# A fused attention and two-mixture kernel: the widest score tiles contract over all 128 rows of the array, and VectorE makes all low parts of the first mixture's weights

## The chip, the cores and the metric

The kernel runs on one core of a Trainium2 chip. A core has a matrix engine (PE; its weight loads are shown apart as PEld), three engines that work on tiles in on-chip memory (VectorE is DVE, ScalarE is ACT, GpSimd is POOL) and SyncE (SP), which here issues most of the transfers. The metric is the device time of one execution in microseconds; lower is better. The clock of the matrix engine has two levels: a granted clock of 1.00 in the profile is 2.4 GHz, 0.50 is 1.2 GHz.

## The reference

Three layers follow one another:

```python
# attention: q, k, v are (4, 8, 576, 64); blocks of 64 positions, a block sees itself and those before it
scores = (q @ k.T) / 8, masked to block_i >= block_j
attn = exp(scores - max) / (sum + 1e-9);  x = attn @ v        # -> x is (2304, 512)
# first mixture: rows with x @ w_skip > 0 go to the best of 8 experts by x @ w_gate
y = relu(x @ w1[e]) @ w2[e];  x = x + gate * y                # 512 -> 1024 -> 512
# second mixture: all rows through all 4 experts, weighted by normalised domain_probs
out = sum over e of p[:, e] * (relu(x @ w1[e]) @ w2[e])
```

All is float32 outside. Inside, an operand is split into a high part (rounded to a narrower form) and a low part (what the rounding left), and a product is three matmuls: high by high, high by low, low by high.

## The kernel before, in words

The program has three stages, which a hand-written order fixes (the scheduler is off: each engine runs its instructions as the code records them).

**Attention** runs over 8 units u, each a batch and a group of four heads. A unit's q is split into the tiles `QH` and `QL`, its k into `KH` and `KL`, each 128 partitions by 2 by 576: the heads of even number lie in partitions 0 to 63, those of odd number in 64 to 127, and the axis of length 2 is `h // 2`. So the contraction of one head, over 64 values, uses 64 of the 128 rows of the array. The score rows of a head are cut into five row tiles rt = 0 to 4; tile rt has 64 + 128 rt columns, so rt = 4 is the widest, with all 576. `score` makes one group: four heads for rt < 2, two heads for rt = 2 or 3, and one head for rt = 4. Where a group has two or four heads, their matmuls are issued in pairs, one on the lower and one on the upper 64 rows. For rt = 4 there is one head in a group, as two halves of 288 columns with three matmuls each, and a mask matmul of 64 columns: seven matmuls, all on the same 64 rows. Four such groups make 28 matmuls in a unit, 224 in all.

After `score`, VectorE takes the row maxima and ScalarE the exponentials (`E`). Two ways then turn `E`: for rt = 1 and 3 PE transposes it (`tp`, L303) and ScalarE and VectorE split it; for rt = 0, 2 and 4 ScalarE rounds `E` to `HL` (L309), GpSimd subtracts the low part (L310), and SyncE's queue issues a transposing transfer to `eT` (L311). Products with v (L335 to L337) follow some groups later, by a table of lags. While unit u is scored, the next unit's q, k and v are split, a few steps at a time: the string `SO` sets the order (J, K, Q on ScalarE; V on VectorE; q, k, v, the low parts `QL`, `kl`, `vl`, on GpSimd; a dot ends a step). Unit 0 has its own string, `S0`.

**The first mixture** (`m1`) goes through 8 experts. An expert's weights come as 8 pieces of 128 by 1024 (four of w1, then four of w2) into raw buffers; `sp` splits a piece as soon as it is its turn: the engines come from the table `SPE`, whose pair names the engine of the high part and that of the low part. In each expert ScalarE makes all high parts; VectorE makes the low parts of pieces 0 to 4 and 6, GpSimd those of pieces 5 and 7 (L635). A piece's raw buffer is free for the next load when its low part is done. On VectorE's queue the subtractions stand ahead of the splits of the transposed activations (`lo`, L658), which PE needs: it has two buffers for transposes (L665), so a third transpose of an expert's tile waits for the first `lo`. GpSimd's queue also issues the writes of the routed rows (L711).

**The second mixture** (`m2`) takes 807 us of the span, and neither edit touches it.

Of the kernel before, what the change touches and what calls it, by code (L numbers as in the profile page):

```python
# [6 lines left out]
F32 = mybir.dt.float32  # L7
F32R = mybir.dt.float32r
# [9 lines left out]
B, H, S, D = 4, 8, 576, 64  # L18
# [34 lines left out]
class Kernel:  # L53
# [5 lines left out]
    R3 = 4, 2  # L59
    CM = 6  # L60
    XO = 0
    S0 = "Qa0213b...V.v"
    XP = 2
    XB = 4
    YL = 5, 0
# [6 lines left out]
    LT = 99  # L72
    XQ = 3
    FT = (10,)
    SPE = ("AV", "AV", "AV", "AV", "AV", "AP", "AV", "AP")
    SB = 3
    PU, W2, X2 = 4, 1, 2
    ORD = "OSMDRTVPUE"
# [24 lines left out]
    PW = 2  # L103
    PM = 1
    HV = ((7, 0),)
    SO = "J..K..Q.Vq..k...v"

    def __init__(self, tc, q, k, v, wr, w11, w12, w21, w22, dp, out):
        self.tc, self.nc = tc, tc.nc
# [3 lines left out]
    def consts(self, cp, ac):  # L113
        nc, self.cp = self.nc, cp
        self.ident = cp.tile([128, 128], F32, name="ident")
        make_identity(nc, self.ident)

        self.maskl = ac.tile([128, 128], F32R, name="maskl")
        self.maskr = ac.tile([128, 64], F32R, name="maskr")
        nc.vector.memset(self.maskl.bitcast(F32), 0.0)  # L120
        nc.vector.memset(self.maskr.bitcast(F32), 1.0)
        for p in (0, 64):
            nc.vector.memset(self.maskl.bitcast(F32)[p:p + 1, 0:64], -1e9)
        self.ones = ac.tile([128, 128], BF16, name="ones")
        nc.vector.memset(self.ones, 1.0)
        tri = ac.tile([128, 128], F32, name="tri")
        nc.vector.memset(tri, 1.0)
        nc.gpsimd.affine_select(out=tri, in_=tri, pattern=[[1, 128]], base=-1, channel_multiplier=-1,
                                compare_op=ALU.is_ge, fill=0.0)
        self.tri = ac.tile([128, 128], BF16, name="tri16")  # L130
        nc.vector.tensor_copy(self.tri, tri)
        self.iota = ac.tile([128, 5, E1], F32, name="iota")
        self.plan = [(w, i, e, c) for e in range(E1) for i, w in enumerate((self.w11, self.w12)) for c in range(4)]
        self.plan += [(w, i, 0, c) for c in range(2) for i, w in enumerate((self.w21, self.w22))]
        self.raw1, self.done1, self.w, self.room = [], 0, [], self.RB
        self.hist = ac.tile([128, E1 + 1], BF16, name="hist")
        self.base = ac.tile([128, E1 + 1], BF16, name="base")
        nc.vector.memset(self.hist, 0.0)
        nc.vector.memset(self.base, 0.0)
        for e in range(E1 + 1):  # L140
            if e < E1:
                nc.gpsimd.memset(self.iota[:, :, e:e + 1], float(e - E1))
            nc.gpsimd.memset(self.base[0:1, e:e + 1], float(e * N))
        self.w9 = ac.tile([128, 4, E1 + 1], F32, name="w9")
        nc.sync.dma_start(self.w9, self.wr)
        self.tok = cp.tile([128, NT], I32, name="tok")
        nc.gpsimd.iota(self.tok, pattern=[[128, NT]], base=0, channel_multiplier=1)
        self.cnt = cp.tile([128, E1], I32, name="cnt")
        self.beg = cp.tile([128, E1], I32, name="beg")
        self.ful = cp.tile([128, E1], I32, name="ful")  # L150
        self.row = cp.tile([128, self.CM, E1], I32, name="row")

    def attention_consts(self, cp, kp):
        nc = self.nc
        self.vh, self.vl, self.kh, self.kl = [], [], [], []
        for i in range(2):
            for x, xs in (("h", self.kh), ("l", self.kl)):
                xs.append(kp.tile([128, 2, S], F32R, name=f"k{x}{i}"))
        for i in range(3):
            t = cp.tile([128, 5, 4, D + 1], F16, name=f"vh{i}")  # L160
            nc.gpsimd.memset(t[:, :, :, D:D + 1], 1.0)
            for h in range(4):
                nc.gpsimd.memset(t[64 - 64 * (h % 2):128 - 64 * (h % 2), 4 - 4 * (h % 2), h, D:D + 1], 0.0)
            self.vh.append(t)
            self.vl.append(cp.tile([128, 5, 4, D], BF16, name=f"vl{i}"))
# [18 lines left out]
    def split_unit(self, u):  # L184

        nc = self.nc
        qr, kr, vr = self.raws.pop(u)
        QH = self.qk.tile([128, 2, S], F32R, name="QH")
        QL = self.qk.tile([128, 2, S], F32R, name="QL")
        KH, KL = self.kh[u % 2], self.kl[u % 2]  # L190
        vh, vl = self.vh[u % 3], self.vl[u % 3]
        self.units[u] = (QH, QL, KH, KL, vh, vl)
        V = nc.vector
        what = {
            "Q": lambda: nc.scalar.copy(QH, qr),
            "q": lambda: (V if self.QV else nc.gpsimd).tensor_tensor(QL, qr, QH.bitcast(F32), ALU.subtract),
            "V": lambda: V.tensor_copy(vh[:, :, :, 0:D], vr),
            "v": lambda: (V if self.VV else nc.gpsimd).tensor_tensor(vl, vr, vh[:, :, :, 0:D], ALU.subtract),
        }
        if u:  # L200
            what["J"] = lambda: nc.scalar.mul(kr, kr, 0.125)
            what["K"] = lambda: nc.scalar.copy(KH, kr)
            what["k"] = lambda: nc.gpsimd.tensor_tensor(KL, kr, KH.bitcast(F32), ALU.subtract)
        else:
            for x, y, i in (("0", "2", slice(0, 1)), ("1", "3", slice(1, 2))):
                what[x] = lambda i=i: V.tensor_scalar(KH[:, i], kr[:, i], 0.125, None, ALU.mult)
                what[y] = lambda i=i: V.scalar_tensor_tensor(KL[:, i], kr[:, i], 0.125, KH[:, i].bitcast(F32),
                                                             ALU.mult, ALU.subtract)
        for x in self.SO if u else self.S0:
            if x == ".":  # L210
                yield
            elif x in "ab":
                i = "ab".index(x)
                (V if i else nc.gpsimd).tensor_tensor(QL[:, i], qr[:, i], QH[:, i].bitcast(F32), ALU.subtract)
            else:
                what[x]()

    def score(self, item, g):

        nc = self.nc  # L220
        u, rt, heads = item
        QH, QL, KH, KL, vh, vl = self.units[u]
        R = 128 if rt else 64
        r0 = 64 + 128 * (rt - 1) if rt else 0
# [9 lines left out]
        for j in range(per):  # L234
            h = heads[g0 + j]
            k0 = 0 if h % 2 else S - n
            if rt == 4:
                outs = [(sp[:, c, 0:288], 288 * c, 288) for c in range(2)]
                views.append(sp[:, :, 0:288])
            elif rt < 2:  # L240
                outs = [(sp[:R, h % 2, (h // 2) * n:(h // 2) * n + n], 0, n)]
                views.append(outs[0][0])
            else:
                outs = [(sp[:, h % 2, 0:n], 0, n)]
                views.append(outs[0][0])
            lm = None if not rt else (len(outs) - 1 if h % 2 else 0)

            p, hp = slice(64 * (h % 2), 64 * (h % 2) + 64), h // 2
            ops = []
            for i, (o, c0, w) in enumerate(outs):  # L250
                c0 += k0
                q, k = (p, hp, slice(r0, r0 + R)), (p, hp, slice(c0, c0 + w))
                ops += [(o, QH[q], KH[k], True, False), (o, QH[q], KL[k], False, False),
                        (o, QL[q], KH[k], False, i != lm)]
                if i == lm:
                    ops.append((o[:, w - 64:w] if h % 2 else o[:, 0:64], self.maskl[p], self.maskr[p], False, True))
            todo.append(ops)
        for two in range(0, per, 2):
            for ops in zip(*todo[two:two + 2]):
# [12 lines left out]
        for j in range(per):  # L272
# [3 lines left out]
            c = heads[j] % 2 * 2 + heads[j] // 2 if rt < 2 else j  # L276
# [448 lines left out]
    def sp(self, n, upto):  # L725
# [3 lines left out]
        for _ in range(n):  # L729
            m = self.done1  # L730
            if m >= min(upto, len(self.plan)):
# [4 lines left out]
            self.w[-1] += self.w_split(self.wp[0 if j < 3 else 1], f"{j}{m % 2}", self.plan[m][1], self.raw1[m],  # L736
                                       [en[c] for c in self.SPE[m % 8]])
            self.done1 += 1
# [407 lines left out]
```

## Time and profile before

| | us |
|---|---|
| runs | 1251.07, 1239.67, 1247.24 (median 1247.24) |
| profiled execution | 1245.87, of which the span is 1244.3 |

| stretch of the span, us | what runs | PE busy | DVE | ACT | POOL | granted clock |
|---|---|---|---|---|---|---|
| 42 to 215 | attention, past its start | 159.83 | 111.43 | 125.35 | 112.73 | 0.84 |
| 215 to 245 | end of attention, routing | 15.77 | 21.48 | 10.33 | 12.38 | 0.81 |
| 245 to 437 | first mixture | 164.00 | 100.22 | 92.25 | 55.53 | 0.95 |
| 437 to 1244 | second mixture | 780.27 | 567.42 | 258.06 | 422.54 | 0.99 |

Busy times are those of the engine in the stretch. PE's matmuls overlap and their ends are modelled, so a busy PE need not be one at its peak: how fast it goes is read from the distance between the starts of two matmuls, and from the granted clock. A busy figure beside a granted clock of 0.50 is time at 1.2 GHz.

### The profile page before, as it was taken

The page shows a single profiled execution, that of the slowest core. Times are in us where ns is not written, and L with a number is a line of the kernel's source. Part 1 is how long each engine was busy: PE and PEld are TensorE (multiplying, and loading weights), DVE is VectorE, ACT ScalarE, POOL GpSimd, SP SyncE. Part 2 cuts the span into 40 slices and gives each one's busy share as a digit, 9 for nine tenths or more (in the row PEclk, how much of TensorE's full clock was granted, in tenths as well). Part 3 has the DMA queues.
Part 4 walks back from the last instruction along what each step waited for, and adds up shares of the span by engine and source line. Part 5 has one row for each costly group of instructions (what it writes and reads, how often), then busy time and mean ns, then how long its engine had stood idle before and what let it go on. Part 6 is the DMA issues. An engine that isn't in the chain of part 4 may idle for free.

```text
span 1244.3 us, 21122 instructions
## 1 busy us (share of the span) xinstructions
PE 1145.9 (92%) x8105; PEld 1020.2 (82%) x8105; DVE 821.7 (66%) x1294; ACT 510.6 (41%) x900; POOL 627.2 (50%) x577
## 2 busy tenths in 40 slices
PE   4989999587898869999999999999999999999998
PEld 4878888576787758898998888988888888888887
DVE  4667566674434676766667766667876777667675
ACT  4887657365434553223232232323333232333321
POOL 4867665333112356554555445455755545555552
PEclk8898769798999979999999999999999999999999
DMA  5988648898553441111111111111411111111101
GB/s 180 207 187 191 170 104 162 236 331 291 165 182 100 137 153 52 51 35 35 34 52 37 49 35 35 51 35 58 129 52 51 52 52 51 35 51 52 35 1 68
DMA packets 129882, 123.89 MB, mean 100 GB/s; under 512 B 65965, under 2 KB 98733, under 8 KB 129744
## 3 DMA queue, kind: packets, MB, share of 16 engines
q1 hardware_dynamic: 127024, 117.48, 33.1%
q0 software_dynamic: 2720, 4.64, 1.1%
q8 instruction: 79, 1.29, 0.4%
q14 instruction: 59, 0.48, 0.1%
HBM read 91.83 MB, written 19.43 MB: 89 GB/s over the span
## 4 chain that ended last, share of the span: by engine, by line
PE 45%; DVE 9%; issue 5%; ACT 4%; POOL 2%; DMA 0%; SPq 0%; POOLq 0%; DVEq 0%; ACTq 0%
PE yp L641 9%; PE yp L643 9%; PE yp L642 8%; PE hp L642 6%; PE hp L643 6%; PE hp L641 6%; DVE acc L961 3%; DVE tl L874 2%; ACT hh L906 2%; DVE C L899 2%; ACT vh L870 1%; POOL C L899 1%; POOL p L899 1%; PE tp L820 1%; DVE u L899 0%
## 5 line engine op out<-in xcount | busy, mean ns | idle before, releaser
L906 ACT ACTIVATE hh<-C 128x512 fp32r<-128x512 f32 (+1 forms) x128 | 87.8, 686 | 434.5 <-DVE C L899 369.8
L641 PE MATMUL yp<-vh,hh 128*128 128x512 f32 x576 | 228.9, 397 | 11.0 <-ACT hh L906 11.0
L961 DVE SCALAR_TENSOR_TENSOR acc<-yp,p,acc 128x512 f32<-128x512 f32 x270 | 196.5, 741 | 56.5 <-PE yp L643 56.5
L643 PE MATMUL yp<-vh,hl 128*128 128x512 f32 x576 | 227.4, 395 | 0.3 <-DVE hl L907 0.3
L642 PE MATMUL yp<-vl,hh 128*128 128x512 f32 x576 | 227.6, 395 | 0.0
L907 DVE SCALAR_TENSOR_TENSOR hl<-C,hh 128x512 fp32r<-128x512 f32 (+1 forms) x128 | 120.9, 944 | 116.6 <-ACT hh L906 116.6
L899 POOL TENSOR_TENSOR p<-u,p 128x384 f32<-128x384 f32 (+1 forms) x64 | 60.2, 941 | 204.1 <-ACT p L896 204.1
L643 PEld LDWEIGHTS yp<-vh,hl 128*128 128x128 f32 x576 | 108.2, 188 | 31.9 <-DVE hl L907 8.2
L641 PEld LDWEIGHTS yp<-vh,hh 128*128 128x128 f32 x576 | 108.9, 189 | 27.5 <-ACT hh L906 14.5
L899 POOL TENSOR_TENSOR C<-u,p 128x384 f32<-128x384 f32 (+1 forms) x64 | 53.2, 831 | 148.0 <-ACT p L896 95.1
L642 PEld LDWEIGHTS yp<-vl,hh 128*128 128x128 f32 x576 | 108.9, 189 | 12.4
L642 PE MATMUL hp<-xsl,th 128*128 128x256 f32 (+1 forms) x384 | 113.6, 296 | 0.0
L643 PE MATMUL hp<-xsh,tl 128*128 128x256 f32 (+1 forms) x384 | 113.5, 296 | 0.0
L641 PE MATMUL hp<-xsh,th 128*128 128x256 f32 (+1 forms) x384 | 113.4, 295 | 0.0
L896 ACT COPY p<-hp 128x256 f32<-128x256 f32 (+1 forms) x192 | 74.5, 388 | 91.1 <-PE hp L643 91.1
L310 POOL TENSOR_TENSOR HL<-E,HL 128x640 bf16<-128x640 f32 (+2 forms) x39 | 66.0, 1704 | 54.8 <-ACT HL L309 45.5
L899 DVE TENSOR_TENSOR C<-hp,p 128x256 f32<-128x256 f32 (+1 forms) x128 | 57.5, 449 | 52.9 <-POOL p L899 52.9
L877 POOL TENSOR_TENSOR vl<-r,vh 128x1024 fp32r<-128x1024 f32 x31 | 91.3, 2945 | 0.0
L874 DVE TENSOR_TENSOR tl<-t,th 128x512 fp32r<-128x512 f32 x32 | 87.0, 2718 | 0.8 <-ACT th L872 0.8
L270 DVE TENSOR_REDUCE m<-s 128x1 f32<-128x576 f32 (+3 forms) x80 | 64.9, 819 | 26.8 <-PE s L261 26.2
L277 ACT ACTIVATE E<-s,m 128x320 f32<-128x320 f32 (+4 forms) x160 | 75.8, 532 | 15.1 <-DVE m L270 13.8
L641 PE MATMUL hp<-xdh,dh 128*128 128x256 f32 (+1 forms) x256 | 76.2, 297 | 1.9 <-ACT xdh L826 1.2
(199 smaller groups left out, 3095.5 us busy)
## 6 DMA issues: line engine op xcount, KB each, us to landing
r<-in_w_dram SPq DMA_DIRECT2D x128, 512.0 KB, 4.3
XN<-x SPq DMA_DIRECT2D x18, 256.0 KB, 7.1
x<-XN SPq DMA_DIRECT2D x18, 256.0 KB, 3.3
vr<-in_v_dram SPq DMA_DIRECT2D x7, 640.0 KB, 8.0
xg<-XS SPq DMA_DIRECT2D x16, 257.0 KB, 4.3
out_dram<-acc SPq DMA_DIRECT2D x16, 256.0 KB, 2.0
qr<-in_q_dram SPq DMA_DIRECT2D x7, 576.0 KB, 5.5
kr<-in_k_dram SPq DMA_DIRECT2D x7, 576.0 KB, 6.5
```

What stands on the lines that cost most here:

```text
L277: nc.scalar.activation(e, views[j], AF.Exp, bias=m[:R, c:c + 1])
L310: (nc.vector if item[:2] in self.HV else nc.gpsimd).tensor_tensor(HL[:R, w:2 * w].bitcast(BF16), Et[:R, 0:w], HL[:R, 0:w], ALU.subtract)
L641: nc.tensor.matmul(out, lhsT=ah, rhs=bh, start=start, stop=False)
L642: nc.tensor.matmul(out, lhsT=ah, rhs=bl, start=False, stop=False)
L643: nc.tensor.matmul(out, lhsT=al, rhs=bh, start=False, stop=stop)
L874: V.tensor_tensor(tl[:, 0:2], t[:, 0:2], th[:, 0:2].bitcast(F32), ALU.subtract)
L877: P.tensor_tensor(vl, r2, vh.bitcast(F32), ALU.subtract)
L896: nc.scalar.copy(t, product(a, b))
L899: add = lambda e, o, x, y: e.tensor_tensor(o, x, y, ALU.add)
L906: nc.scalar.activation(hh[:, i:i + 2], C[:, i:i + 2], AF.Relu)
L907: V.scalar_tensor_tensor(hl[:, i:i + 2], C[:, i:i + 2], 0.0, hh[:, i:i + 2].bitcast(F32), ALU.max, ALU.subtract)
L961: nc.vector.scalar_tensor_tensor(a, yp, self.p[:, n, e:e + 1], a, ALU.mult, ALU.add)
```

## The change

Two edits. **The widest tiles (rt = 4).** Each unit keeps, beside `QH` and `QL`, two tiles `q4h` and `q4l` of 128 partitions by 4 heads by 128 positions, with the last 128 positions of q: a head's 64 values stand in its own half of the partitions, and the other half holds zeros. There are two sets, for units in turn; GpSimd zeroes them once at the start and then copies, for each unit, the four pieces (steps X and x of the strings, each with two copies of 64 by 2 by 128). The rt = 4 matmuls take `q4h` and `q4l` as stationary operand and all 128 partitions of k as moving one; the rows of the other head meet zeros. Their mask matmul contracts over 128 rows too (`mask4`, with -1e9 in row 0 alone). The number, order and columns of the matmuls stay.

**The first mixture.** `SPE` now names VectorE for the low parts of pieces 5 and 7.

```diff
-    S0 = "Qa0213b...V.v"
+    S0 = "Qa0213b...V.vXx"
-    SPE = ("AV", "AV", "AV", "AV", "AV", "AP", "AV", "AP")
+    SPE = ("AV", "AV", "AV", "AV", "AV", "AV", "AV", "AV")
-    SO = "J..K..Q.Vq..k...v"
+    SO = "J..K..Q.Vq..k...vX.x"
...
-        for p in (0, 64):
-            nc.vector.memset(self.maskl.bitcast(F32)[p:p + 1, 0:64], -1e9)
+        self.mask4 = ac.tile([128, 128], F32R, name="mask4")
+        nc.vector.memset(self.mask4.bitcast(F32), 0.0)
+        for t, p in ((self.maskl, 0), (self.maskl, 64), (self.mask4, 0)):
+            nc.vector.memset(t.bitcast(F32)[p:p + 1, 0:64], -1e9)
...
+        self.q4 = []
+        for i in range(2):
+            self.q4.append([kp.tile([128, 4, 128], F32R, name=f"q4{x}{i}") for x in "hl"])
+            for t in self.q4[i]:
+                nc.gpsimd.memset(t.bitcast(F32), 0.0)
...
+        def last(x):
+            for a in range(2):
+                p = slice(64 * a, 64 * a + 64)
+                nc.gpsimd.tensor_copy(self.q4[u % 2][x][p].rearrange("p (c a) s -> p a c s", a=2)[:, a], (QH, QL)[x][p, :, S - 128:S])
+
+        what["X"], what["x"] = lambda: last(0), lambda: last(1)
...
-                q, k = (p, hp, slice(r0, r0 + R)), (p, hp, slice(c0, c0 + w))
-                ops += [(o, QH[q], KH[k], True, False), (o, QH[q], KL[k], False, False),
-                        (o, QL[q], KH[k], False, i != lm)]
+                if rt < 4:
+                    q, k = (p, hp, slice(r0, r0 + R)), (p, hp, slice(c0, c0 + w))
+                    qh, ql, ml, mr = QH[q], QL[q], self.maskl[p], self.maskr[p]
+                else:
+
+                    k = (slice(0, 128), hp, slice(c0, c0 + w))
+                    (qh, ql), ml, mr = (t[:, h] for t in self.q4[u % 2]), self.mask4, self.maskr
+                ops += [(o, qh, KH[k], True, False), (o, qh, KL[k], False, False), (o, ql, KH[k], False, i != lm)]
                 if i == lm:
-                    ops.append((o[:, w - 64:w] if h % 2 else o[:, 0:64], self.maskl[p], self.maskr[p], False, True))
+                    ops.append((o[:, w - 64:w] if h % 2 else o[:, 0:64], ml, mr, False, True))
```

What this does to the order of two queues follows. First GpSimd, around the split of the next unit in the middle of the attention (`QL`, `kl`, `vl`: the low parts of the next unit; `HL`: the low parts of E of the unit being scored). Before:

```order
L310 TENSOR_TENSOR HL<-E,HL 64x256
L196 TENSOR_TENSOR QL<-qr,QH 128x1152
L203 TENSOR_TENSOR kl_128<-kr,kh_127 128x1152
L198 TENSOR_TENSOR vl_151<-vr,vh_145 128x1280
L310 TENSOR_TENSOR HL<-E,HL 128x640 x2
```

And of the change:

```order
L211 TENSOR_TENSOR kl_131<-kr,kh_130 128x1152
L206 TENSOR_TENSOR vl_162<-vr,vh_156 128x1280
L220 COPY q4h_134<-QH 64x2x128 x2
L220 COPY q4l_135<-QL 64x2x128 x2
L329 TENSOR_TENSOR HL<-E,HL 128x640 x2
L329 TENSOR_TENSOR HL<-E,HL 128x1152 x2
```

Four copies stand between `vl` and the next `HL`, in each of the 8 units; nothing else moved on this queue in the attention.

Second VectorE, in the second expert of the first mixture (`w2l` and `w1l` are low parts of weights, r the raw pieces, `lo` the low parts of transposed activations). Before:

```order
L635 TENSOR_TENSOR w2l<-r_4256,w2h 128x1024
L635 TENSOR_TENSOR w2l<-r_4268,w2h 128x1024
L658 TENSOR_TENSOR lo<-tp,hi 128x512 x3
L635 TENSOR_TENSOR w1l<-r_4280,w1h 128x1024
L635 TENSOR_TENSOR w1l<-r_4532,w1h 128x1024
```

And of the change:

```order
L654 TENSOR_TENSOR w2l<-r_4299,w2h 128x1024
L654 TENSOR_TENSOR w2l<-r_4305,w2h 128x1024
L654 TENSOR_TENSOR w2l<-r_4311,w2h 128x1024
L654 TENSOR_TENSOR w2l<-r_4317,w2h 128x1024
L677 TENSOR_TENSOR lo<-tp,hi 128x512 x3
```

Four subtractions instead of two stand ahead of the three `lo`; GpSimd's two are gone from its queue, in each of the 8 experts.

## Rows read from the trace of the kernel before

**Rows 1.** Windows, attention: us, each engine's busy time (instructions), clock, DMA share, GB/s.

```profile
42.00:215.00 173.00, 159.83 (x2154) 145.80 (x2152) 111.43 (x246) 125.35 (x231) 112.73 (x72) 0.84 0.80 170
```

**Rows 2.** Windows, same columns, stretches at one granted clock in the attention.

```profile
28.50:35.30 6.80, 6.46 (x45) 5.81 (x45) 3.50 (x6) 4.50 (x7) 4.35 (x3) 0.50 0.29 60
35.40:42.20 6.80, 6.80 (x75) 6.20 (x73) 4.04 (x8) 6.77 (x15) 5.48 (x3) 0.50 0.81 183
66.10:69.50 3.40, 1.82 (x18) 1.75 (x19) 1.16 (x2) 3.10 (x7) 3.33 (x2) 1.00 1.02 137
124.20:127.50 3.30, 3.19 (x36) 2.87 (x35) 2.09 (x3) 3.17 (x6) 3.30 (x2) 1.00 0.65 252
127.60:134.30 6.70, 6.70 (x83) 6.29 (x79) 2.22 (x8) 3.63 (x5) 2.67 (x3) 0.50 0.63 139
151.40:161.70 10.30, 10.30 (x66) 9.08 (x64) 3.56 (x5) 4.77 (x7) 2.80 (x2) 0.50 0.37 73
161.70:175.20 13.50, 13.50 (x171) 12.47 (x172) 9.23 (x38) 10.54 (x21) 6.57 (x9) 0.50 0.56 99
```

**Rows 3.** Windows of the score matmuls (L261) alone: PE, PEld, clock, DMA, GB/s.

```profile
124.20:127.50 3.30, 1.83 (x13) 1.45 (x11) 1.00 0.65 252
151.40:161.70 10.30, 5.73 (x21) 5.06 (x21) 0.50 0.37 73
```

**Rows 4.** Timeline, PE, widest tiles: start, duration (us), line, out<-in, rows*columns, xcount.

```profile
49.27 0.29 PE L261 MATMUL s<-kl,QH 64*128 64x288 f32 x1
49.40 0.29 PE L261 MATMUL s<-kh,QL 64*128 64x288 f32 x1
...
149.44 0.44 PE L261 MATMUL s<-kl,QH 64*128 64x288 f32 x1
149.69 0.44 PE L261 MATMUL s<-kh,QL 64*128 64x288 f32 x1
```

**Rows 5.** Timeline, PE, second mixture, matmuls on 128 rows at full clock.

```profile
601.31 0.28 PE L642 MATMUL hp<-xsl,th 128*128 128x256 f32 x1
601.42 0.28 PE L643 MATMUL hp<-xsh,tl 128*128 128x256 f32 x1
```

**Rows 6.** Timeline, GpSimd, attention; in brackets the idle time before, and its releaser.

```profile
10.12 1.90 POOL L214 TENSOR_TENSOR QL<-qr,QH 128x576 fp32r<-128x576 f32 x1 [4.68 <-DMA vr<-in_v_dram]
...
24.96 0.53 POOL L484 MEMSET z<- 128x514 f32 x1
...
64.13 0.66 POOL L310 TENSOR_TENSOR HL<-E,HL 64x256 bf16<-64x256 f32 x1 [2.25 <-PE og L337]
...
76.56 1.40 POOL L310 TENSOR_TENSOR HL<-E,HL 128x640 bf16<-128x640 f32 x1 [2.71 <-ACT HL L309]
...
126.34 2.78 POOL L310 TENSOR_TENSOR HL<-E,HL 128x640 bf16<-128x640 f32 x2
133.15 4.72 POOL L310 TENSOR_TENSOR HL<-E,HL 128x1152 bf16<-128x1152 f32 x2 [4.03 <-ACT HL L309]
```

**Rows 7.** Timeline, GpSimd and VectorE, first mixture, low parts of w2.

```profile
266.41 4.74 POOL L635 TENSOR_TENSOR w2l<-r,w2h 128x1024 fp32r<-128x1024 f32 x2
...
266.55 5.68 DVE L635 TENSOR_TENSOR w2l<-r,w2h 128x1024 fp32r<-128x1024 f32 x1 [1.02 <-ACT w2h L634]
...
338.71 2.35 DVE L635 TENSOR_TENSOR w2l<-r,w2h 128x1024 fp32r<-128x1024 f32 x2
```

**Rows 8.** Timeline, PE, first mixture, matmuls that follow an idle time.

```profile
272.99 0.63 PE L665 MATMUL tp<-ident,h 128*128 128x128 f32 x4 [3.42 <-DVE lo L658]
...
313.05 0.63 PE L665 MATMUL tp<-ident,h 128*128 128x128 f32 x4 [2.65 <-DVE lo L658]
...
341.81 0.63 PE L665 MATMUL tp<-ident,h 128*128 128x128 f32 x4 [0.17 <-DVE lo L658]
...
343.35 0.50 PE L702 MATMUL yp<-w2l,hi 128*128 128x512 f32 x1 [0.68 <-POOL w2l L635]
...
432.45 1.20 PE L702 MATMUL yp<-w2h,lo 128*128 128x512 f32 x4 [2.11 <-DVE lo L658]
```

## The prediction

> **What bounds the kernel now.** I read the page's busy shares first, then windows by stage, then the slices of granted clock in the attention, then the timelines of the engines at the places the change touches. PE is busy 92% of the span by the page, but the two stages that the change touches are the ones where it is not simply full. In the attention from 42 to 215 us it is busy 159.8 of 173 us [rows 1], more than ScalarE (125.4), GpSimd (112.7) or VectorE (111.4), so PE sets the pace; and it has a mean granted clock of only 0.84. That is the reader's first point: a busy PE there is partly a PE at 1.2 GHz. The second mixture, two thirds of the span, is untouched.
>
> Where is the clock low? [Rows 2] list the stretches. At 66.1 PE is idle nearly half of the time (1.82 of 3.40 us), with ScalarE full, and the clock falls behind it; such a fall opens most units. The fall at 127.6 is of another kind: in the stretch ahead of it PE is busy 3.19 of 3.30 us, and more than half of that is score work [rows 3], of the widest tiles. The long slow spell is of that kind too: between 151.4 and 161.7 PE has no idle time at all, 21 of its 66 matmuls are those of the widest tiles [rows 2, 3], and the clock stays at 1.2 GHz; likewise from 28.5 to 35.3. What these stretches share is matmuls that go one after another over 64 of the 128 rows, the other half of the array doing nothing. The other narrow scores go in pairs, one on each half. So I read it thus: what lifts or holds the clock is work over the array's rows, and a lone matmul on 64 rows gives half of it. From 161.7 to 175.2 PE was busy all the time without wide tiles in most of it and the clock rose only at the end, so other work (transposes, products of few columns) lifts it slowly too.
>
> **The widest tiles, step by step.** The order on PE stays. A matmul of 288 columns on 64 rows starts 0.13 us after the one before at full clock and 0.25 us at half [rows 4]. On 128 rows, 256 columns take 0.11 us [rows 5], in proportion to columns (0.124 us for 288); so the rows cost PE nothing, and I enter zero for all 224 matmuls. What can be won is time at 1.2 GHz. Time moved from half to full clock shrinks by 1 - 0.13/0.25 = 0.48 while PE is the bound. Three stretches hold wide tiles before or during slowness:
> - start: 35.4 to 42.2, behind a stretch full of wide tiles. The clock would be up when it begins: 6.8 x 0.48 = 3.3 us.
> - the fall at 127.6: with the rows full ahead of it, it does not come: 6.7 x 0.48 = 3.2 us.
> - the long spell: it begins with an idle PE, as before, and wide tiles come from 149 on. I let the clock rise at 154.9, after about half of them; then 6.8 us of the stretch to 161.7 and the 13.5 us behind it go at full clock: 20.3 x 0.48 = 9.7 us. Bounds: nothing, if wide tiles can hold a clock but not lift it, and (10.3 + 13.5) x 0.48 = 11.4 us if it rises with the first ones.
>
> Sum 16.2 us. Such spells lie elsewhere in other executions, so the sum is that of this one; the three runs differ by 11 us, which one long spell more or less would make.
>
> A rule speaks against this reading. The Trainium skill, in "TensorE: Matmul & The Clock Gate", Part 1, says that a hardware block sets the clock by how busy the PE has been lately. By it, rows do not count, a lone 64-row stream is as busy as a full one, and the sum would be 0 instead of 16.2 us. The rows at 151.4 do not sit well with it, since a PE without idle time stayed at 1.2 GHz there.
>
> **GpSimd's copies.** At the start come four memsets of 128 by 512. One of 128 by 514 takes 0.53 us [rows 6]; 2.1 us stand in front of the first `QL`, before which GpSimd was idle 4.68 us for a transfer. Nothing. Per unit come four copies of 64 by 256. No row has a copy of this size; the nearest is the subtraction of 64 by 256 with two inputs, 0.66 us [rows 6], which I take as the price: 2.6 us a unit. The lower bound is half of the memset's 0.53 us, for half the columns: 0.27 us, or 1.1 us a unit. They stand between `vl` and the first `HL` of 128 by 640. What hides them: GpSimd waited 2.71 us for ScalarE there at 76.56; in the unit at 126.34 it did not wait, but the next `HL` then waited 4.03 us [rows 6], so the queue catches up within the unit. What is late for a while is `HL`, its transposing transfer and, behind it on SyncE's queue, the loads of a unit two ahead; the products that read `eT` come groups later. I enter 0, with 2.6 us a unit as price if the cover fails.
>
> **The first mixture.** GpSimd loses 16 subtractions, VectorE gains 16. On VectorE one costs 2.35/2 = 1.18 us while GpSimd is quiet, but 5.68 us at 266.55, when GpSimd had just started two of its own that last 4.74 us [rows 7]: VectorE's ended about a microsecond after GpSimd's. So VectorE did not merely share; it stood still. Three experts of the eight show this, and PE paid each time: 3.42, 2.65 and 2.11 us [rows 8], waiting for a `lo` queued behind the stalled subtraction. After the change VectorE does all four in 4 x 1.2 us, without a stall; followed through the queue, `lo` comes some 2.5 us earlier in these three. The first lies in a stretch where the next expert's weights are still being loaded, so I give it 0; the other two give 2.5 and 2.1 us.
>
> The other five pay. In two (at 341.81, and one more of its kind) VectorE starts late, and `lo` moves back by two subtractions, 2.35 us; PE, which waited 0.17 us there, waits about 2.4, and is spared the wait of 0.68 us for GpSimd's piece [rows 8] and the refilling behind it: +1.6 and +1.5 us. In three VectorE waits for ScalarE between the pieces, only one subtraction is added to the path, and part of it is covered: +0.35 each. Sum: -4.6 + 3.1 + 1.0 = -0.5 us. Bounds: -7.6 if only the gains arrive (the first one too), +4.1 if only the costs.
>
> GpSimd's queue also issues the routed rows' writes behind these pieces; they get earlier, and nobody waits for them but the second mixture's first load, which follows the last expert, where the queue is empty.
>
> **Sum.** 1245.87 (the profiled execution, 1.4 us under the median) - 16.2 - 0.5 = 1229.2; I forecast 1229 us, 1.5% below the median.
>
> **Rivals.**
> 1. *The clock does not answer*: zeros do not count as work, or rows never did. For it: the slow spell from 161.7 without wide tiles; against it: the fall at 127.6 out of a busy stretch. Time: 1245.9 - 0.5 = 1245, to 1250 with part of the copies uncovered.
> 2. *VectorE becomes the wait in every expert of the first mixture*: four subtractions in a row ahead of each `lo`, 8 x 1.6 = 12.8 us, and no stall is cured because the stalls had another cause. Against it: the end of the 5.68 us beside GpSimd's. With the clock's gain: 1245.9 - 16.2 + 12.8 = 1243.
> 3. *Slower: GpSimd is late in the attention.* The copies push `HL`, and SyncE's queue stands behind a transfer that waits for `HL`, so that PE idles for products, and the idle PE lets the clock fall as at 66.1. For it: no wait ahead of `HL` at 126.34. Price: 7 units x 2.6 = 18.5 us, and the clock's gain is gone: 1264 us. It decides once the four copies exceed what GpSimd waits in a unit, 2.71 us at 76.56 before the first `HL` or 4.03 at 133.15 before the third, about 0.7 to 1.0 us a copy.
>
> **Chances.** Forecast 0.66, rival 1 0.18, rival 2 0.09, rival 3 0.07. The forecast's own range is 1219 (1245.9 - 3.3 - 3.2 - 11.4 - 7.6 = 1220.4, and a microsecond for where the spells lie) to 1239 (the long spell not shortened). The range of 8 in 10 reaches to rival 1's upper end, 1250, and leaves out rival 3. One per cent, 12.5 us, is about what a measurement of this kernel can tell from no change: under 1234.8 counts as faster. Most of the forecast's case lies there, the part with a long spell left does not: faster 0.55, same 0.38, slower 0.07.
>
> **What would show it.** Granted clock in the attention above 0.84, no fall out of a stretch of wide tiles, and no stretch at 1.2 GHz that outlasts a unit's wide tiles; falls that open a unit, as at 66.1, still there. The rt = 4 matmuls 0.13 us apart, on 128 rows. In the first mixture no VectorE subtraction over 2 us, and the three PE waits gone, with new ones of one to two microseconds in the experts that start late. If the clock's slices look as before, the first reading is wrong; if PE waits for `eT` or `HL`, the copies are the cause.

## The result, and the profile after

The changed kernel takes **1234.11 us** (median of 20 runs, 1226.67 to 1239.73) against 1248.44 us of the kernel before (20 runs beside it, 1234.37 to 1257.14). The ratio is 0.9898, with a 95% interval from 0.9873 to 0.9922: 14 us faster. The medians are over all runs; the ratios leave out, on both sides, runs more than 1.5% above the fastest of their kernel, of which only the kernel before and the one with 64 rows below (one run) have any. Forecast were 1229 us, with a range from 1219 to 1250. The profiled execution took 1235.50 us, its span is 1233.9; before it was 1245.87 and 1244.3, so that these two executions lie 10.4 us apart.

First the stages. A stage ends here with the last score matmul, with the first transposes of the first expert and with those of the second mixture; the windows of the kernel before (its first one ends with the last score), then of the changed one (the second one stands beside [rows 1]), with the columns of [rows 1]:

```profile
18.00:211.97 193.97, 176.45 (x2232) 160.16 (x2230) 123.00 (x264) 142.29 (x259) 129.83 (x83) 0.81 0.75 164
212.00:244.71 32.71, 18.48 (x323) 17.04 (x322) 22.86 (x99) 12.13 (x25) 12.38 (x16) 0.81 0.84 226
244.71:443.57 198.86, 164.29 (x1016) 144.52 (x1017) 105.16 (x103) 95.06 (x126) 56.78 (x32) 0.95 0.60 198
443.57:1244.30 800.73, 780.27 (x4488) 692.65 (x4488) 562.47 (x810) 255.24 (x480) 421.28 (x405) 0.99 0.16 51
```

```profile
18.00:198.30 180.30, 155.83 (x2228) 145.06 (x2229) 119.34 (x261) 139.17 (x253) 141.45 (x113) 0.90 0.78 173
42.00:215.00 173.00, 149.30 (x2253) 139.30 (x2254) 114.36 (x267) 126.12 (x234) 128.34 (x104) 0.91 0.86 186
198.30:236.11 37.81, 22.14 (x326) 20.01 (x322) 23.50 (x101) 13.27 (x29) 12.51 (x16) 0.74 0.87 211
236.11:431.48 195.37, 164.87 (x1017) 145.02 (x1017) 107.99 (x119) 95.31 (x126) 17.36 (x16) 0.93 0.61 202
431.48:1233.90 802.42, 781.27 (x4488) 694.08 (x4488) 563.06 (x810) 255.62 (x480) 421.31 (x405) 0.99 0.16 51
```

Read the boundaries as a ledger. The scores end 13.7 us earlier (212.0, now 198.3). The tail behind them, which ends the attention and routes the rows, takes 37.8 us instead of 32.7 and gives 5.1 back. The first mixture is 3.5 us shorter, the second 1.7 longer: 13.7 - 5.1 + 3.5 - 1.7 = 10.4. The 1.7 us are no effect of the change: in the thirteen executions profiled of this study the second mixture, the same code in all, takes between 800.6 and 803.5 us. From 42 to 215 us the mean granted clock rose from 0.84 [rows 1] to 0.91, while PE's busy time there fell by 10.5 us.

Where the clock changed is seen in stretches of the changed kernel, to be held against [rows 2]:

```profile
28.60:35.30 6.70, 5.80 (x88) 5.43 (x89) 5.54 (x12) 6.06 (x9) 5.58 (x7) 1.00 0.36 88
38.80:42.20 3.40, 1.64 (x17) 1.23 (x14) 2.18 (x5) 3.40 (x6) 3.40 (x3) 1.00 1.16 168
42.20:49.00 6.80, 5.50 (x54) 5.25 (x55) 3.17 (x6) 4.22 (x8) 6.80 (x4) 0.50 1.07 195
62.70:66.10 3.40, 1.72 (x20) 1.28 (x16) 1.75 (x5) 3.40 (x7) 1.45 (x2) 1.00 1.09 231
113.90:117.30 3.40, 1.88 (x20) 1.47 (x17) 1.75 (x6) 3.40 (x7) 3.08 (x4) 1.00 0.94 171
124.20:134.30 10.10, 9.68 (x169) 9.25 (x171) 6.60 (x16) 8.73 (x18) 9.02 (x9) 1.00 0.50 124
137.80:141.20 3.40, 1.70 (x16) 1.38 (x17) 0.88 (x2) 3.40 (x6) 2.40 (x1) 1.00 1.07 156
141.20:148.00 6.80, 6.80 (x59) 6.72 (x59) 3.26 (x6) 2.50 (x6) 6.64 (x7) 0.50 0.99 266
148.00:168.50 20.50, 17.20 (x288) 15.72 (x286) 16.07 (x47) 17.49 (x32) 13.14 (x13) 1.00 0.66 154
165.10:168.50 3.40, 1.98 (x21) 1.66 (x19) 2.64 (x6) 3.38 (x7) 3.40 (x2) 1.00 0.93 247
168.50:171.90 3.40, 3.40 (x41) 3.34 (x41) 1.36 (x3) 1.59 (x4) 3.21 (x3) 0.50 0.31 104
```

From 28.6 to 35.3 and from 124.2 to 134.3 the clock is at 1.00, where it stood at 0.50 from 28.5 and from 127.6 on. The five rows of 3.4 us at 1.00 are those ahead of a fall: PE is busy 1.64 to 1.98 us in each, with ScalarE full (3.38 us or more). So the falls that open a unit are still there, and none comes out of a busy stretch. The fall at 141.2 is the one that opened the long spell before; now it lasts 6.8 us. The two rows of the kernel before:

```profile
144.60:151.40 6.80, 6.80 (x58) 6.37 (x58) 3.29 (x7) 2.22 (x5) 5.02 (x2) 0.50 0.92 284
144.60:175.30 30.70, 30.70 (x293) 28.02 (x293) 16.17 (x48) 17.63 (x33) 14.48 (x13) 0.50 0.58 132
```

The first 6.8 us of this spell hold nearly the same work in both kernels (58 and 59 matmuls, PE without idle time), and in both the last seven score matmuls of it are the unit's first wide ones, here from 146.03 on:

```profile
146.03 0.59 PE L280 MATMUL s<-kh,q4h 128*128 128x288 f32 x1
```

On 128 rows the clock rises behind them, at 148.0; on 64 rows it stayed at 1.2 GHz for another 23.9 us.

The second stretch that now keeps its clock holds much score work too, as before [rows 3]; of the score matmuls alone:

```profile
124.20:134.30 10.10, 4.92 (x56) 4.40 (x58) 1.00 0.50 124
```

The changed instructions themselves: the wide matmuls in PE's timeline; then the copies, which the profile calls CAST, in the view of their line (duration least, median, largest in ns; first and last start; shape; and who waited for them: us, times); then VectorE's w2l, in the view of the tile; then PE's waits in the first mixture.

```profile
148.83 0.29 PE L280 MATMUL s<-kl,q4h 128*128 128x288 f32 x1
148.96 0.30 PE L280 MATMUL s<-kh,q4l 128*128 128x288 f32 x1
```

```profile
L220 POOL CAST q4h<-QH x16: 391/400/884, 17.3 to 177.9; 64x256 fp32r<-64x256 f32 x16
L220 POOL CAST q4l<-QL x16: 392/397/402, 18.6 to 178.8; 64x256 fp32r<-64x256 f32 x16
...
  POOL HL L329: 4.8, 3
```

```profile
L654 DVE TENSOR_TENSOR w2l<-r,w2h x32: 1215/1218/1226, 238.8 to 417.7; 128x1024 fp32r<-128x1024 f32 x32
```

```profile
271.32 0.55 PE L702 MATMUL hp<-w1h,hi 128*128 128x256 f32 x1 [3.61 <-PEq L789]
277.34 0.58 PE L702 MATMUL hp<-w1l,hi 128*128 128x256 f32 x1 [5.47 <-issue]
331.31 0.63 PE L684 MATMUL tp<-ident,h 128*128 128x128 f32 x4 [2.41 <-DVE lo L677]
387.78 0.63 PE L684 MATMUL tp<-ident,h 128*128 128x128 f32 x4 [1.42 <-DVE lo L677]
```

The wide matmuls start 0.13 us apart on 128 rows, as on 64 [rows 4]. A copy takes 0.40 us; `HL` waited for the copies three times, 4.8 us together. None of VectorE's 32 subtractions for w2 stands still any more, and the three waits of PE that [rows 8] show for `lo` (3.42, 2.65 and 2.11 us) are gone; two new ones are there.

### The profile page after: what moved, and what is told of

Same layout as the page of the kernel before. It is cut to its first block, busy times and chain, and to the rows that moved or that the text cites. A ratio compares the mean times of both kernels' runs of the same rounds, so it can differ in the third digit from the quotient of the medians.

```text
span 1233.9 us, 21146 instructions
## 1 busy us (share of the span) xinstructions
PE 1130.4 (92%) x8105; PEld 1009.7 (82%) x8105; DVE 824.8 (67%) x1312; ACT 510.7 (41%) x900; POOL 602.7 (49%) x597
## 4 chain that ended last, share of the span: by engine, by line
PE 45%; DVE 9%; issue 8%; DMA 5%; ACT 4%; POOL 2%; POOLq 0%; another core or an unknown queue 0%; SPq 0%; DVEq 0%; ACTq 0%
PE yp L660 9%; PE yp L662 9%; PE yp L661 8%; PE hp L661 6%; PE hp L662 6%; PE hp L660 6%; DMA xi<-XS 4%; DVE acc L980 4%; DVE tl L893 2%; ACT hh L925 2%; DVE C L918 2%; ACT vh L889 1%; POOL C L918 1%; DMA XN<-ys,xg 1%; POOL p L918 1%
## 5 line engine op out<-in xcount | busy, mean ns | idle before, releaser
L660 PEld LDWEIGHTS yp<-vh,hh 128*128 128x128 f32 x576 | 109.1, 189 | 27.4 <-ACT hh L925 14.3
L730 POOL DMA_INDIRECT XN<-ys,xg x10 | 13.0, 1299 | 155.4 <-DVE ys L729 106.1
L296 ACT ACTIVATE E<-s,m 128x320 f32<-128x320 f32 (+4 forms) x160 | 76.0, 532 | 10.4 <-DVE m L289 9.5
```

Of the source, the lines that this page charges most:

```text
L296: nc.scalar.activation(e, views[j], AF.Exp, bias=m[:R, c:c + 1])
L660: nc.tensor.matmul(out, lhsT=ah, rhs=bh, start=start, stop=False)
```

## The experiments

**Which part, and rows or copies?** Four kernels ran beside one another (the kernel before took 1249.47 us there, 35 runs).

*The rows without the low parts:*

```diff
-    SPE = ("AV", "AV", "AV", "AV", "AV", "AV", "AV", "AV")
+    SPE = ("AV", "AV", "AV", "AV", "AV", "AP", "AV", "AP")
```

> The changed kernel with the first mixture's low parts of pieces 5 and 7 back on GpSimd: the wide tiles on 128 rows alone. Theory (the gain is the granted clock in the attention, worth about 11 of the 14 us): about 1237 us, ratio 0.991, and in the first mixture VectorE subtractions of about 5 us are back. Rival (the first mixture gave most of it): 1245 or more.

Measured: 1234.94 us, ratio 0.9931 (0.9896 to 0.9967), with VectorE subtractions of 5.57, 4.99 and 5.55 us back.

*The low parts without the rows* (the same line the other way round, in the kernel before):

> The kernel before with all low parts of the first mixture on VectorE, the score tiles as before. Theory (worth 0.5 to 3.5 us, since three waits of PE go and smaller ones come): 1245 to 1248 us, ratio 0.997 to 1.000, attention clock as before. Rival (this edit is the larger one): 1238 or less.

Measured: 1246.87 us, ratio 1.0014 (0.9970 to 1.0059). Alone, this part can't be told from no change. In the execution profiled no subtraction stalls (the longest takes 1.23 us) and the first mixture takes 189.4 us, 9.5 less than before, but the stretch ahead of it, from the last score to the first expert, takes 40.4 instead of 32.7.

*Everything of the change, but the wide matmuls read only the head's own 64 rows of the new tiles:*

```diff
-                    k = (slice(0, 128), hp, slice(c0, c0 + w))
-                    (qh, ql), ml, mr = (t[:, h] for t in self.q4[u % 2]), self.mask4, self.maskr
+                    k = (p, hp, slice(c0, c0 + w))
+                    (qh, ql), ml, mr = (t[p, h] for t in self.q4[u % 2]), self.maskl[p], self.maskr[p]
```

> The changed kernel, with all its copies and its first mixture, but the wide tiles contract over the head's own 64 rows of the new tiles (and of k and the mask). Theory (rows of the array hold the clock): scores end some 10 us later than in the changed kernel, spells of 10 us or more at 1.2 GHz out of busy stretches are back, 1244 to 1247 us, ratio about 0.998. Rival (the new tiles or the moved order gave it, not the rows): 1234 us and a clock as in the changed kernel.

Measured: 1241.78 us, ratio 0.9969 (0.9922 to 1.0016). The copies, the tiles and the low parts are all there, and most of the gain is not: the kernel takes 6.8 us more than the rows alone and 9.5 more than the small numbers below, which ran beside it. The clock of all runs says it most plainly. The mean granted clock of the whole kernel is 0.950 here (12 runs), 0.950 in the kernel before (35; 0.954 in the 20 that its ratio takes) and 0.950 with the low parts alone (12), the three with 64 rows; it is 0.965 with the rows alone and 0.964 with small numbers (12 each), and 0.963 in the 20 runs of the changed kernel. So it is the rows that the matmuls run over; whether they count in the weight loads or in the matmuls, which both got 128, the runs don't separate. Not all came as expected: the time is under 1244 us, the scores end at 202.1, only 3.8 us behind the changed kernel (7.5 behind the rows alone and 10.8 behind the small numbers), and of the long spells only that of the start is back, 20.5 us from 18.8 on. From 42 to 215 us this execution has no spell over 6.8 us, and its clock there is 0.93, above the 0.91 of the changed kernel; one execution shows the difference only at its start:

```profile
42.00:215.00 173.00, 151.51 (x2223) 137.21 (x2220) 114.27 (x266) 126.61 (x233) 128.90 (x104) 0.93 0.84 182
```

*Small numbers instead of the zeros* (the tiles start as 1.37e-20; each score takes up the other head's k times that, which is lost in float32):

```diff
-                nc.gpsimd.memset(t.bitcast(F32), 0.0)
+                nc.gpsimd.memset(t.bitcast(F32), 1.37e-20)
```

> The changed kernel with 1.37e-20 in place of the zeros beside q, which adds nothing that can be seen to the scores but gives every cell of the array a product to make. Theory (instructions on 128 rows count, whatever the values): 1234 us and the same clock. Rival (zeros count for less): more granted clock in the attention and 1230 us or less.

Measured: 1232.29 us, ratio 0.9924 (0.9886 to 0.9962), as the changed kernel, and the same clock (0.964 and 0.963). Rows that meet zeros do as much for the clock as rows that meet a small constant; operands of full size were not tried.

Within an execution, the start of the attention shows the rows most plainly, since the copies and the low parts are the same in all three kernels. The same windows, first of the kernel with 64 rows (the second row counts its score matmuls alone: PE, PEld, clock, DMA, GB/s):

```profile
28.60:39.20 10.60, 10.27 (x91) 9.70 (x93) 6.12 (x12) 9.10 (x16) 8.87 (x8) 0.50 0.31 72
28.60:39.20 10.60, 8.18 (x55) 7.64 (x57) 0.50 0.31 72
```

then of the changed kernel, and of that with small numbers a longer one:

```profile
28.70:39.20 10.50, 8.68 (x150) 7.89 (x150) 8.69 (x15) 9.86 (x19) 9.48 (x9) 1.00 0.38 84
```

```profile
18.00:36.00 18.00, 14.20 (x128) 12.70 (x128) 10.15 (x18) 13.77 (x21) 14.18 (x16) 1.00 0.35 107
```

With 64 rows PE is busy 10.27 of 10.60 us, mostly with scores, and the clock stays at 0.50; on 128 rows it is less busy and at 1.00. The spread of the runs fits. Of the 35 runs of the kernel before, 22 lie above 1245 us, and so do 5 of 12 with copies on 64 rows and 8 of 12 with the low parts alone; of the 44 of the changed kernel, the rows alone and the small numbers none does (highest 1239.73). The executions profiled of the kernel before and of the low parts alone (1245.87 and 1247.32 us) have a spell of 30.7 us each; the ten profiled on 128 rows have none over 10.3 us before their last score. So what the rows take away are, it seems, the executions with such spells; the other runs were not profiled.

**Can the falls that open a unit be had as well?** ScalarE does three passes of about 1.16 us there, for the scaling of k (L209) and the casts of k and q, while PE waits for its exponentials. Two kernels move one pass to VectorE; two others deal with the tail. Here the kernel before took 1250.0 us (29 runs).

```diff
-            what["J"] = lambda: nc.scalar.mul(kr, kr, 0.125)
+            what["J"] = lambda: V.tensor_scalar(kr, kr, 0.125, None, ALU.mult)
```

> The changed kernel with k's scaling by 0.125 (units 1 to 7) on VectorE instead of ScalarE. Theory A: what is left of the stretches at 1.2 GHz in the attention opens at the start of a unit, where TensorE idles 1.2 to 1.7 us for exps of ScalarE, which has three casts of 1.17 us each there; with one cast less per unit at least three of the five openings after 60 us vanish, the granted clock of 42 to 215 us rises from 0.91 to 0.94 or more, the first expert's first matmul comes 3 to 6 us earlier than 236.1, and the whole takes about 1229 to 1232 us (ratio to the kernel before 0.984 to 0.988). Theory B: the clock opens its falls at the unit's seam whatever ScalarE does (VectorE's row maxima come later by the 1.2 us it now spends): clock 0.90 to 0.92 there and 1233 to 1237 us. Theory C: the attention gains, and the tail between the last scores and the first expert gives it back, as in the kernel with small numbers: scores end at 192 to 195 us, the first expert still at 235 to 236.

Measured: 1239.43 us, ratio 0.9965 (0.9930 to 1.0000), slower than the changed kernel's 0.9898. The mean clock of 42 to 215 us is 0.92, so theory A fails; the time lies above what theory B gave, too. The scores end at 202.6 instead of 198.3. The rows of this kernel suggest why: VectorE's scaling in all units, then VectorE, GpSimd and PE in the timeline.

```profile
L209 DVE TENSOR_SCALAR kr<-kr x7: 870/2320/3641, 16.5 to 159.5; 128x1152 f32<-128x1152 f32 x7
```

```profile
84.42 2.91 DVE L209 TENSOR_SCALAR kr<-kr 128x1152 f32<-128x1152 f32 x1
110.84 3.64 DVE L209 TENSOR_SCALAR kr<-kr 128x1152 f32<-128x1152 f32 x1
165.57 3.98 DVE L205 CAST vh<-vr 128x1280 f16<-128x1280 f32 x1
```

```profile
81.99 4.72 POOL L329 TENSOR_TENSOR HL<-E,HL 128x1152 bf16<-128x1152 f32 x2 [1.95 <-ACT HL L328]
111.48 2.37 POOL L329 TENSOR_TENSOR HL<-E,HL 128x1152 bf16<-128x1152 f32 x1
166.22 2.63 POOL L204 TENSOR_TENSOR QL<-qr,QH 128x1152 fp32r<-128x1152 f32 x1
```

```profile
172.11 1.75 PE L322 MATMUL tp<-ident,E 128*128 128x128 f32 x7 [3.42 <-ACT lgs L408]
```

The pass costs ScalarE 1.16 us. VectorE took 0.87 to 3.64 for it, median 2.32, and ended 0.6 us after an instruction of GpSimd did: at 87.33 after 86.71, at 114.48 after 113.85. In the trace all seven end 0.61 to 0.63 us after the end of the GpSimd instruction that ran or began beside them, the shortest too. So about 0.6 us is what the pass itself takes (an estimate from these ends; none ran alone), and the rest is standing still, some 10 us in seven units. The cast of v, pushed beside two other subtractions, took 3.98 us where 0.82 is its median in the changed kernel. It is the stall of [rows 7] again, now on an engine whose row maxima ScalarE and PE wait for. That these stalls are the whole loss is not shown.

The other kernel moves the cast of q:

```diff
-            "Q": lambda: nc.scalar.copy(QH, qr),
+            "Q": lambda: (V.tensor_copy if u else nc.scalar.copy)(QH, qr),
```

> The changed kernel with the cast of q's high part (units 1 to 7) on VectorE instead of ScalarE. Theory A (ScalarE's casts at the unit's start idle TensorE and open the falls): as for the kernel with k's scaling moved, but this cast is the last of the three, so it takes away less of the exps' wait: one to three openings vanish, 1230 to 1234 us. Theory B (the seam itself): no opening vanishes, 1233 to 1237 us.

Measured: 1242.67 us, ratio 0.9983 (0.9937 to 1.0028): worse than both said, and 6 of its 12 runs lie above 1245 us though the wide tiles are on 128 rows, so that more than the rows decides about such runs. No case for moving work to VectorE here.

**The tail.** The executions profiled of the changed kernel (two), of the rows alone (two) and of the small numbers end their scores between 191.4 and 198.3 us, and the first expert begins at 235.0 to 236.1 us in four of them and at 239.7 in one; the earliest scores (191.4) bring it no earlier (235.4). In none of the thirteen executions profiled does it begin before 235.0. To tell whether the transposing transfers are the cause, the last unit's third row tile is turned on PE:

```diff
-    PE_T = ((7, 0), (7, 1))
+    PE_T = ((7, 0), (7, 1), (7, 2))
```

> The changed kernel with the last unit's third row tile turned on TensorE instead of by transfers on SyncE's queue (3.98 us each, four at the end of the attention). Theory T: the tail gives back what the attention gained because TensorE waits there for those transfers (1.54 us at 202.2) and the clock then falls to 1.2 GHz; with TensorE turning the tiles the attention's last matmul comes 3 to 6 us earlier, the granted clock of 215 to 245 us rises from 0.58 to over 0.65, and the whole takes 1228 to 1231 us (ratio 0.983 to 0.987). Rival: the tail is bound by the routing's chain (scatter, gather of the first expert's rows, the router's sums over all tokens) and by the transfers of the weights, so that the first expert still starts at 235 to 237 us: 1233 to 1236 us.

Measured: 1228.15 us (6 runs), ratio 0.9878 (0.9816 to 0.9941). The clock from 215 to 245 us is 0.68 instead of 0.58, as theory T has it, but the first expert begins at 238.3. Both edits together, with k's scaling on VectorE:

> Both together: k's scaling on VectorE and the last unit's third row tile turned on TensorE. If theories A and T both hold: the sum of the two, 1223 to 1228 us (ratio 0.979 to 0.983), the first expert's first matmul at 227 to 231 us. If the tail is bound by transfers and the routing's chain: the first expert at 234 to 236 us and 1231 to 1235 us. If only the tail's turning counts: as the kernel with that alone, within 1.5 us.

Measured: 1235.85 us, ratio 0.9936 (0.9900 to 0.9972): 3.6 us under the kernel with the scaling alone, but above all three ranges that were expected; the first expert begins at 240.4. Since six runs are few, three kernels ran once more on one chip (the kernel before 1244.07 us, 18 runs), none of them edited further:

> The changed kernel once more, beside the next two on one chip, so that differences of half a per cent can be told: 1231 to 1237 us, ratio to the kernel before 0.987 to 0.993, no run above 1243 us.

> The rows' part alone (low parts of the first mixture shared with GpSimd as before), beside the changed kernel. Theory that the split of the low parts is worth 4 to 6 us in the first mixture (its length times its granted clock was 185.7 us with it shared and 181.7 with all on VectorE): 3 to 6 us above the changed kernel, the VectorE subtraction over 5 us back. Rival, the split is worth nothing by the clock (the prediction's 0.5 us): within 1.5 us of the changed kernel.

> The kernel with the last unit's third row tile turned on TensorE, beside the changed kernel, because its time (1228, six runs) was lower but its profile showed the first expert no earlier. If the tail's granted clock counts: 3 to 6 us under the changed kernel. If the six runs were chance and the routing's chain binds the tail: within 1.5 us of it.

Measured: the changed kernel 1230.19 us (7 runs, 1227.70 to 1234.35; ratio 0.9902, 0.9863 to 0.9940), just under the range that was expected; the rows alone 1233.14 (12 runs; 0.9937, 0.9905 to 0.9969), with VectorE subtractions of 5.67 and 5.27 us back, 3.0 us above it, the foot of what was expected of a split that counts; the last turns on PE **1224.92** (6 runs, 1221.44 to 1229.23; 0.9860, 0.9819 to 0.9900), 5.3 us under the changed kernel. That is the fastest version of this study. Its tail, below that of the changed kernel beside it, and then the two first mixtures in the same order:

```profile
194.39:234.98 40.59, 21.85 (x325) 19.89 (x322) 23.33 (x101) 13.26 (x29) 12.51 (x16) 0.72 0.83 198
```

```profile
200.30:235.52 35.22, 20.27 (x333) 18.25 (x332) 23.27 (x103) 12.14 (x27) 9.71 (x14) 0.79 0.67 208
```

```profile
234.98:429.75 194.77, 164.69 (x1016) 145.52 (x1017) 108.03 (x119) 95.32 (x126) 17.31 (x16) 0.93 0.60 202
235.52:426.75 191.23, 164.59 (x1016) 144.98 (x1017) 108.03 (x119) 95.31 (x126) 17.30 (x16) 0.94 0.62 206
```

The clock is higher and the DMA engines have less to do, but the first expert begins no earlier in these two executions (235.0 and 235.5 us). The time came out as the theory had it, the place did not. Between these two executions, 5.2 us apart, 3.5 us lie in the first mixture and 2.2 in the second, less 0.5 at the first expert's start, and the edit touches neither mixture; the kernel with small numbers has both as short (190.5 and 800.6 us) without the edit. So where the difference of the medians comes from stays open, and so does what keeps the first expert from starting before 235 us.

## Why the prediction was right, and where it was not

**The clock answers to rows: right.** The rule of busy time alone would have given nothing; with copies and low parts in place, 64 rows gave 1241.78 us and a mean clock of 0.950, 128 rows (small numbers, beside it) 1232.29 us and 0.964. What the Trainium skill says in "TensorE: Matmul & The Clock Gate", Part 1, that the clock goes by how busy the PE is, holds for the falls that open a unit, where PE is idle about half of the time (1.64 to 1.98 of 3.40 us busy); the stretch from 28.6 to 39.2 differs, busy and slow on 64 rows, less busy and fast on 128, and there the measurement decides.

**The three terms of the clock: the sum near, two sizes by luck.** The start: 35.4 to 42.2 was forecast at full clock and is. But the spell there opened earlier, at 18.3 instead of 21.7, and a new one of 6.8 us came at 42.2 behind a half idle PE: 10.3 + 6.8 us at 1.2 GHz instead of 20.5, 3.4 us less, worth 1.6 us instead of 3.3. The fall at 127.6 did not come: right. The long spell: the clock rose at 148.0, after the first wide tiles, which is the upper bound of 11.4 us and not the rise after half of them; a fall at 168.5 that was not foreseen took 3.4 us back. So 30.7 us became 6.8 and 3.4, 20.5 us less, by 0.48 the 9.8 us for which 9.7 stood in the sum: two errors that cancel. The short falls changed as well, one longer by 3.4 us, three gone. In all, up to the last score, 74.2 us at 1.2 GHz became 37.5; by 0.48 that would be 17.6 us, and 13.7 arrived. Part of the rest went into waiting: PE's waits between 18 us and the last score grew from 17.2 to 26.1 us.

**The step that was wrong: the attention's gain was carried to the end of the kernel undiminished.** The prediction has no term for the tail. It took 5.1 us back: in it PE is busy 22.1 of 37.8 us, the clock fell from 0.81 to 0.74, and the first expert starts no earlier than 235.0 us, however early the scores end. The kernel with small numbers shows it at its largest: clock 0.97 up to 190 us and scores done at 191.4, then a tail of 44 us at 0.62.

```profile
18.00:190.00 172.00, 147.75 (x2198) 137.31 (x2199) 117.51 (x255) 138.39 (x249) 142.20 (x114) 0.97 0.81 177
191.40:235.38 43.98, 26.44 (x323) 24.39 (x322) 23.02 (x101) 13.22 (x29) 12.51 (x16) 0.62 0.78 191
```

A row of the kernel before could have warned: from 215 to 245 us PE was busy 15.8 of 30 us. The tails of all thirteen executions say more. They take from 32.7 to 44.0 us, and the longer ones tend to have the lower clock: length times clock stays between 26.5 and 30.9 us. From the shortest to the longest it grows by 0.8 us; had 11.3 us of idle time at 1.2 GHz merely been added, it would have grown by half of them, 5.6. The end of the scores alone does not set the length, since with the low parts alone the scores end at 213.6 and the tail still takes 40.4 us, at 0.67. So it seems that the tail lost in clock a part of what the attention had won. No run set the tail's clock by itself; this is an argument from the rows, not shown.

**GpSimd's copies: right.** 0.40 us each, 1.6 us a unit, between the bounds of 1.1 and 2.6; they delayed `HL` by 4.8 us in all, and rival 3, the slower side, did not come: PE has no wait for `HL` or for an `eT` that a transfer brings in the units. It does wait for the `eT` that VectorE writes behind PE's own transposes, 5.5 us in seven waits (2.5 in four before), which the copies do not feed. One for a transfer's `eT`, 1.54 us, stands at 202.2, in the tail. **224 matmuls at no cost: right**, 0.13 us apart as before.

**The first mixture: mechanism right, size too small.** Forecast were 0.5 us, 3.5 came in the profiled executions, and about 3 us lie between the rows alone and the whole change, twice on one chip (1233.14 and 1230.19; 1234.94 and, with small numbers, 1232.29; ranges that overlap). In the executions profiled the stage takes 197.0 to 198.9 us in the three with the low parts shared, 189.4 to 195.4 in the ten with all on VectorE. By the waits: the two stalls counted gave 4.8 us (2.65 + 2.11; forecast 4.6). The first stall, entered at 0, gave 1.1: its 3.42 us went, and the waits behind it grew from 6.75 us (2.10 and 4.65) to 9.08. So these two took back two thirds of it, not all; that they are waits for the weights, the views do not show (they name PE's own queue and `issue`). The two before:

```profile
281.93 0.36 PE L683 MATMUL hp<-w1h,hi 128*128 128x256 f32 x1 [2.10 <-PEq L770]
287.43 0.58 PE L683 MATMUL hp<-w1l,hi 128*128 128x256 f32 x1 [4.65 <-issue]
```

The two experts with a late VectorE got their waits, 2.41 and 1.42 us, as forecast; the 1.0 us for three others was not found. Rival 2, VectorE late in every expert, is out with that. Two things are not shown: that the low parts alone are worth 3 us (alone they measured 1.0014, within an interval that holds both), and why the clock of the first mixture went from 0.95 to 0.93; in the ten executions with the same low parts it lies between 0.93 and 0.95. One bound was added up wrong: the gains of 4.6 and 2.5 us make 7.1, not 7.6, which moves the lower end of the range by half a microsecond.

**The total.** 16.7 us were forecast between two executions and 10.4 came; between medians it was 14.3, from a median of before 1.2 us higher than the one the forecast was held to. The 6.3 us that lack between the executions are 2.5 of the attention, 5.1 of the tail and 1.7 of the second mixture (its spread), less 3.0 that the first mixture gave beyond its forecast.

## What to carry to other kernels

Where a profile shows PE busy and its clock at half, look at how many rows its matmuls contract over: unpaired work on 64 rows can be filled up with zeros, here at no PE time (0.13 us from start to start, as before). A gain of clock can be lost in the next stage, where PE waits and its clock falls; look at the busy share and the clock of the stage behind the one you speed up. And before work goes from ScalarE or GpSimd to VectorE, see what GpSimd runs at that moment: here the same move cured stalls in one stage (no subtraction left on GpSimd) and made them in another (GpSimd busy beside it).

## What the runs showed of the hardware

- **Rows count for the clock.** The three kernels with the wide tiles on 64 rows ran at a mean granted clock of 0.950 each, those on 128 rows beside them at 0.964 and 0.965.
- **Zeros count as work.** Rows fed with zeros and rows fed with 1.37e-20 gave the same time within the intervals (0.9898 and 0.9924) and the same clock (0.963 and 0.964).
- **VectorE stands still beside GpSimd, with one input too.** The scaling of 128 by 1152 float32 took from 0.87 to 3.64 us, and each of the seven ended 0.61 to 0.63 us after a GpSimd instruction did; a cast of 128 by 1280 took 3.98 us instead of 0.82. The Trainium skill's "GPSIMD Engine Reference", section 1, has the two engines share their way to the on-chip memory, and names VectorE's instructions with two inputs or in a two-port mode as those that contend; the trace agrees that they contend. Whether these two ran in such a mode the trace does not tell.
